# Toeplitz weights of two channels per load in 32-partition pieces, x loads and transposes moved to the front, and fewer V tasks

## The chip, the cores and the metric

The kernel runs on one core of a Trainium2 chip. The metric is the device time of one execution in microseconds (us). A core has TensorE (PE: matrix products; its weight loads are listed as PEld), VectorE (DVE), ScalarE (ACT), GpSimd (POOL) and SyncE (SP), each with its own instruction stream, and 16 DMA engines that move data between HBM and on-chip memory. Engines meet at semaphores. A DMA is issued from a queue: here mostly SP's, and also ACT's and POOL's. An engine works through its stream in order, so an instruction that waits holds up all that stand behind it. TensorE's clock has two levels, 1.2 and 2.4 GHz; the profile gives the granted clock of a stretch as a share of the higher.

## What is computed

Two independent parts whose outputs stand side by side. Part A is a long convolution over 2048 steps for each of 640 channels; part B is attention with 32 heads of width 20 over 2048 rows.

```python
# part A (S = 2048, D = 640, ks = 4)
k_shift = sum over t of k_pad[:, t:t + S, :] * shift_k[:, ks - 1 - t]
kv = k_shift * v
y = causal convolution of kv with ssm_k along S, for each channel (by FFT in the reference)
a = q * (y + kv * ssm_D)
# part B (H = 32, Dh = 20)
q, k, v = split(x @ wqkv)
p = softmax(q k^T * Dh ** -0.5)
b = (p v) @ wo
out = concatenate([a, b], axis=-1)          # all in bf16
```

## The kernel before

**Recording and queues.** The program is recorded in one Python pass: `Prog.op` and `Prog.dmas` append to an engine's list and derive semaphore waits from the buffers that a step reads and writes (`Buf`). The order of the recording is the order of each engine's stream. All DMAs pass L144, the helper, so the profile shows them under that line.

**Attention.** The work is cut into 512 blocks b: a chunk of 512 queries (qc, 4 of them), a group of four heads (g, 8), a block of 128 keys (kb, 16). For each block `S_task` (L410) makes four score matmuls (L418) into two pairs of PSUM banks out of three (banks 0 to 5), `EXP_task` (L427) takes two exponentials of 128x1024 on ScalarE (L430) into one of eight slots of `P_sb`, and `PV_task` (L437) adds P times V into bank 6 (`OBANK`, L443). After 16 blocks the sum is copied out and an N task (L455) transposes and divides it. After eight groups come T tasks (`OnT_task`, transposes L499) and O tasks (`O_task`, the output product L514).

**The loop** (L720) does for each b: the exponentials of b, the scores of b+1, P times V of b-1, and then side tasks: up to two (one from b = 48 on) from the list `pend`, which is sorted by a due time. In it are the transposes of x (X tasks, `XT_task`, L293), the projections for K and Q (`KQ_task`, L314, 20 matmuls each), the V projections (`V_task`, L333, three for each key block by the table `VZ`: 8, 12 and 12 heads), and the N, T and O tasks. From the start of the loop (`late`) all side tasks share one PSUM bank, 7 (`MISC`); ahead of it X tasks rotate through banks 2 to 5. Every fifth block from 25 on a `kv_task` makes 128 rows of kv on VectorE, from k and v rows loaded by `kst_load` and from `Ctile`, shift_k spread over all partitions. Setup gets `Ctile` on POOL's queue: an element-wise load of shift_k to four partitions, a copy to the scratch `kshT`, and a broadcast load.

**The convolution** runs from b = 124 in blocks that have no task due. It is a product with Toeplitz weights: for one step, called a channel in what follows, `hk_load` (L560) brings 128 rows of 2112 elements from `kext_scratch` (the zero-padded kernel in HBM) to a slot of `HK`. Row p of 32 rows starts p elements later in the same row of `kext`, which makes it a Toeplitz matrix; the four groups X of 32 partitions hold four channels 80 apart. There are 160 steps, five slots (`NHK`), and each slot is loaded again when its last matmul is recorded. A step has 32 matmuls (L594) with 128x128 weights out of its slot. Four steps make a batch, which ends with two copies on VectorE and four matmuls (L615, called z here), and takes six blocks: about 26, 26, 27, 28 and 21 matmuls, then L615. There are 40 batches. The moving operand `KVX` is rearranged on POOL (L571) from `KVr`, which `kvr_load` (L556) brings in twice, from rows of 160 bytes. After 20 batches `A_load` and `A_task` (L625, L632) finish half of part A.

**At the start**, SP loads x in two pieces of 512 rows into two slots of `xst`, ACT's queue issues the weights in ten DMAs (5 chunks, of 160 columns of each of K, Q and V for `b_Wa`, then of 480 for `b_Wb`), and the third and fourth piece of x are issued after the X tasks of a slot are recorded.

## Time and profile before

| what | value |
|---|---|
| median of 3 runs | 1476.86 us (1476.44 to 1484.54) |
| the profiled execution's time | 1481.97 us |
| its span, first to last instruction | 1480.1 us |
| ScalarE busy | 970.8 us, 66% |
| PE busy (matmuls) | 1015.2 us, 69% |
| VectorE busy | 273.5 us, 18% |
| DMA moved | 129.06 MB, mean 87 GB/s |
| mean granted clock | 0.671 |

The profile is one execution. Its views: the chain of work that ended last, followed back from the end; the waits, by engine and by what ended them; busy time by line; busy time in chosen stretches; instructions in order of time. "Idle before" an instruction is time in which its engine did nothing, and the name behind the arrow is what ended it. Matmuls are pipelined, so the sum over lines is more than what PE needs.

### The profile page before, as it was taken

How to read it: one execution, taken by the hardware profiler on the slowest of the kernel's cores; microseconds unless marked ns; L12 is line 12 of the kernel's file. 1: busy time of each engine (PE TensorE's matmuls, PEld its weight loads, DVE VectorE, ACT ScalarE, POOL GpSimd, SP SyncE). 2: the span in 40 equal slices, each digit the busy share in tenths (PEclk: the TensorE clock that was granted, in tenths of full speed). 3: DMA queues.
4: the chain of work that ended last, by engine and by line, in shares of the span. 5: the costliest groups of instructions: out<-in, count | busy, mean ns of one | idle time of the engine just before them, and what ended most of it. 6: DMA issues, size and time to landing. Idle time of an engine off the chain costs nothing.

```text
span 1480.1 us, 24848 instructions
## 1 busy us (share of the span) xinstructions
PE 1015.2 (69%) x11344; PEld 478.6 (32%) x11344; DVE 273.5 (18%) x570; ACT 970.8 (66%) x1027; POOL 123.9 (8%) x100
## 2 busy tenths in 40 slices
...
GB/s 143 159 1 37 88 68 91 94 72 109 72 76 106 106 107 106 106 106 106 116 103 109 104 128 109 107 106 106 106 106 106 106 106 94 83 17 1 1 0 19
DMA packets 70487, 129.06 MB, mean 87 GB/s; under 512 B 21456, under 2 KB 47182, under 8 KB 70382
## 3 DMA queue, kind: packets, MB, share of 16 engines
...
q10 hardware_dynamic: 4000, 2.46, 0.9%
q0 software_dynamic: 1056, 3.44, 0.8%
...
q14 instruction: 16, 0.13, 0.0%
...
## 4 chain that ended last, share of the span: by engine, by line
DMA 45%; PE 23%; ACT 19%; DVE 8%; SPq 3%; issue 1%; ACTq 0%; DVEq 0%
DMA R<-kext_scratch 42%; ACT P_sb L430 19%; PE PS L314 6%; PE PS L594 5%; PE PS L418 4%; PE PS L443 4%; SPq L144 3%; PE PS L514 2%; PE PS L333 2%; DVE R L364 1%; DVE R L362 1%; DVE KT L321 1%; DMA R<-kv_scratch 1%; DVE QT L321 1%; DMA R<-in_B_x_dram 1%
## 5 line engine op out<-in xcount | busy, mean ns | idle before, releaser
L430 ACT ACTIVATE P_sb<-PS 128x1024 bf16<-128x1024 f32 x1024 | 968.3, 1056 | 483.8 <-PE PS L418 474.3
L594 PE MATMUL PS<-R 128*128 128x128 bf16 (+15 forms) x5120 | 297.5, 221 | 215.3 <-DMA R<-kext_scratch 215.3
L594 PEld LDWEIGHTS PS<-R 128*128 128x128 bf16 x5120 | 262.9, 115 | 292.0 <-DMA R<-kext_scratch 223.6
L418 PE MATMUL PS<-QT,KT 20*128 20x512 bf16 x2048 | 273.6, 524 | 109.2 <-ACT P_sb L430 104.6
L443 PE MATMUL PS<-P_sb,V_sb 128*21 128x512 bf16 x2048 | 271.2, 521 | 3.7 <-DVE V_sb L338 2.5
L571 POOL COPY R<-R 32x512 bf16<-32x512 bf16 x80 | 107.2, 1339 | 724.8 <-PE PS L594 714.1
L418 PEld LDWEIGHTS PS<-QT,KT 20*128 20x128 bf16 x2048 | 54.4, 96 | 255.9 <-ACT P_sb L430 203.1
L314 PE MATMUL PS<-R 128*20 128x512 bf16 x1280 | 106.3, 475 | 44.0 <-DVE KT L321 10.9
L607 DVE CAST ZH<-PS 128x256 bf16<-128x256 f32 x40 | 17.0, 424 | 559.8 <-PE PS L594 559.8
L443 PEld LDWEIGHTS PS<-P_sb,V_sb 128*21 128x21 bf16 x2048 | 51.6, 91 | 188.2 <-issue 180.1
L451 DVE CAST OT_sb<-PS 128x512 bf16<-128x512 f32 x32 | 22.1, 691 | 293.6 <-PE PS L443 293.5
L314 PEld LDWEIGHTS PS<-R 128*20 128x20 bf16 x1280 | 32.6, 105 | 95.0 <-issue 29.9
L514 PE MATMUL PS<-Wo_sb,OnT 128*128 128x320 bf16 x160 | 39.0, 401 | 22.9 <-DVE OnT L503 18.3
L333 PE MATMUL PS<-R 128*128 128x240 bf16 (+1 forms) x240 | 35.8, 291 | 16.4 <-DVE V_sb L338 9.2
L321 DVE CAST KT<-PS 128x512 bf16<-128x512 f32 x32 | 22.1, 690 | 61.2 <-PE PS L314 61.2
L333 PEld LDWEIGHTS PS<-R 128*128 128x128 bf16 x240 | 21.3, 109 | 31.8 <-DVE V_sb L338 13.5
L321 DVE CAST QT<-PS 128x512 bf16<-128x512 f32 x32 | 22.1, 690 | 48.4 <-PE PS L314 48.4
L514 PEld LDWEIGHTS PS<-Wo_sb,OnT 128*128 128x128 bf16 x160 | 17.1, 121 | 41.8 <-DVE OnT L503 21.3
L293 PE MATMUL PS<-ident,R 128*128 128x128 bf16 x80 | 9.8, 287 | 26.1 <-DMA R<-in_B_x_dram 22.7
L549 POOL MEMSET R<- 128x2048 bf16 x2 | 3.6, 1804 | 284.3 <-DMA kvr_scratch<-R 284.2
L615 PE MATMUL PS<-ZH,Win 128*128 128x256 bf16 x80 | 23.0, 388 | 6.2 <-DVE ZH L608 6.1
L338 DVE CAST V_sb<-PS 128x240 bf16<-128x240 f32 (+1 forms) x48 | 18.3, 381 | 42.7 <-PE PS L333 42.7
...
## 6 DMA issues: line engine op xcount, KB each, us to landing
R<-kext_scratch SPq DMA_DIRECT2D x160, 528.0 KB
R<-in_A_k_dram SPq DMA_DIRECT2D x15, 640.0 KB, 3.8
R<-in_B_x_dram SPq DMA_DIRECT2D x4, 640.0 KB, 8.9
...
```

Source lines behind the costliest of these rows:

```text
L144: ins = e.dma_start(out, in_)
L314: ins = e.matmul(bank[bk][32 * i:32 * i + DH, :], W_sb[:, cc, off + i * DH:off + (i + 1) * DH], xT[:, cc, c * 512:(c + 1) * 512], start=(c ...
L321: P.op("dve", lambda e: e.tensor_copy(dstT[:, g, c * 512:(c + 1) * 512], bank[bk]), reads=[bkb[bk]], writes=[bd])
L333: ins = e.matmul(bank[bk][:, 0:w], xT[:, cc, kb * 128:(kb + 1) * 128], W_sb[:, cc, 2 * D + h0 * DH:2 * D + h0 * DH + w], start=(cc == 0), ...
L418: ins = e.matmul(bank[bk], KT[32 * u:32 * u + DH, g, kb * 128:(kb + 1) * 128], QT[32 * u:32 * u + DH, g, qc * 512:(qc + 1) * 512], start=T ...
L430: P.op("act", lambda e, pr=pr, s0=s0: e.activation(P_sb[:, pr % NPS, :], PS[:, s0 * 512:s0 * 512 + 1024], ACT.Exp, scale=scale), reads=[bk ...
L443: ins = e.matmul(bank[OBANK][32 * u:32 * u + DH + 1, :], V_sb[:, kb, 4 * g + u, :], P_sb[:, (2 * b + u // 2) % NPS, (u % 2) * 512:(u % 2) ...
L451: P.op("dve", lambda e: e.tensor_copy(OT_sb[:, i, :], bank[OBANK]), reads=[bkb[OBANK]], writes=[b_OT[i]])
L514: ins = e.matmul(bank[bk][:, 0:320], OnT[:, i, cc, :], Wo_sb[:, cc, hf * 320:(hf + 1) * 320], start=(cc == 0), stop=(cc == NCC - 1))
L571: P.op("pool", lambda e, dst=dst, src=src: e.tensor_copy(dst, src), reads=[cv["KVr"]], writes=[cv["KVX"][i]] if X == 3 else [], extra=(cv[ ...
L594: P.op("pe", lambda e, o=o, lhsT=lhsT, rhs=rhs, st=st, last=last: e.matmul(o, lhsT, rhs, start=st, stop=last, skip_group_check=True), read ...
L615: ins = e.matmul(sub(bank[MISC], [[64, 4], [1, n]], o), w, sub(a, [[64, 4], [1, n]]), start=False, stop=True, skip_group_check=True)
```

## The change

1. `HK` has three slots of two channels in place of five of one. `hk_load` is called for a pair, and issues four DMAs of 32 partitions each, whose source leads with the 32 partitions and then the two channels. A slot is loaded again after every second channel. The matmuls read the same columns.
2. All four x loads are issued at the start on SP, into four slots. ACT's queue issues the 160-column weights in three DMAs (K, Q, V), SP the 480-column ones in three after x.
3. The X tasks that are not done ahead of the loop are due in its first three blocks: up to six tasks run in each of these, without a budget. In these blocks (`late` = 1) side tasks alternate between banks 7 and 6, and P times V is held back and then made up, two at a time.
4. `VZ` has two entries (8 and 24 heads) in place of three: 32 V tasks for 48, the second kind with 480 columns.
5. `Ctile` is made on VectorE at b = 16 (`C_task`, four strided copies) from a broadcast load of shift_k into the second `kst` slot; the three POOL DMAs and the scratch `kshT` go. That slot's first k load follows C_task.
6. The first k load is cut at partition 32.

```diff
 HKW = 2112
-NHK = 5
+NHK = 3
...
-        HK_E, KVR_E, KVX_E, Y_E, AST_E = HKW, 64 * 80, 8 * 256, 16 * 320, 2 * 320
-        ph0 = NCC * S + NCC * 1920 + 2 * 4 * D + 2 * 5 * D + KS * D + 2 * D + 2 * D
+        HK_E, KVR_E, KVX_E, Y_E, AST_E = 2 * HKW, 64 * 80, 8 * 256, 16 * 320, 2 * 320
+        ph0 = NCC * S + NCC * 1920 + 4 * 4 * D + 2 * 5 * D + KS * D + 2 * D + 2 * D
...
         W_sb = carve(NCC * 1920).rearrange("p (c n) -> p c n", c=NCC)
-        xst = [carve(4 * D).rearrange("p (t d) -> p t d", t=4) for _ in range(2)]
+        xst = [carve(4 * D).rearrange("p (t d) -> p t d", t=4) for _ in range(4)]
...
         pos[0] = 0
-        HK = [carve(HK_E) for _ in range(NHK)]
+        HK = [carve(HK_E).rearrange("p (s n) -> p s n", s=2) for _ in range(NHK)]
...
         kvr_d = nc.dram_tensor("kvr_scratch", (S, D), BF16).ap()
-        kshT = nc.dram_tensor("kshT_scratch", (KS, D), BF16).ap()
...
         b_Wa, b_Wb, b_Wo, b_D = Buf(), Buf(), Buf(), Buf()
-        b_xst = [Buf(), Buf()]
+        b_xst = [Buf() for _ in range(4)]
...
         b_QT = {(qc, g): Buf() for g in range(NG) for qc in range(4)}
-        b_V = {(kb, z): Buf() for kb in range(NKB) for z in range(3)}
+        b_V = {(kb, z): Buf() for kb in range(NKB) for z in range(2)}
...
-        d_x = [DS("x0"), DS("x1")]
-
-        def x_load(n):
-            P.dma("sp", xst[n % 2], ap(x2, [[D, 128], [128 * D, 4], [1, D]], n * 512 * D), d_x[n % 2],
-                  writes=[b_xst[n % 2]])
-
-        dW = [DS("wa"), DS("wb")]
-        for z, (c0, w, bw) in enumerate(((0, 160, b_Wa), (160, 480, b_Wb))):
-            x_load(z)
-            P.dmas("act", [(ap(W_sb, [list(W_sb.ap[0]), [D, 3], [1, w]], cc * 1920 + c0),
-                            ap(B_wqkv, [[1920, 128], [D, 3], [1, w]], cc * 128 * 1920 + c0)) for cc in range(NCC)],
-                   dW[z], writes=[bw])
+        for n in range(4):
+            P.dma("sp", xst[n], ap(x2, [[D, 128], [128 * D, 4], [1, D]], n * 512 * D), DS("x%d" % n),
+                  writes=[b_xst[n]])
+        for eng, c0, w, bw in (("act", 0, 160, b_Wa), ("sp", 160, 480, b_Wb)):
+            P.dmas(eng, [(ap(W_sb, [list(W_sb.ap[0]), [1920, NCC], [1, w]], z * D + c0),
+                          ap(B_wqkv, [[1920, 128], [128 * 1920, NCC], [1, w]], z * D + c0)) for z in (1, 0, 2)],
+                   DS("w" + eng), writes=[bw])
...
         rot = [0]
-        late = [False]
+        late = [0]
...
         def mbank():
-            if late[0]:
+            if late[0] == 2:
...
             rot[0] += 1
-            return (MISC, 0, 1)[rot[0] % 3]
+            return ((MISC, OBANK, 0, 1)[rot[0] % 4], (MISC, OBANK)[rot[0] % 2])[late[0]]
...
             if late[0]:
-                bk = MISC
+                bk = mbank()
...
                 xbank[0] += 1
-            src = xst[(t // 4) % 2]
+            src = xst[t // 4]
...
                 return ins
-            P.op("pe", pe, reads=[b_xst[(t // 4) % 2], b_ident], writes=[bkb[bk]])
+            P.op("pe", pe, reads=[b_xst[t // 4], b_ident], writes=[bkb[bk]])
...
                 P.op("dve", lambda e: e.tensor_copy(dst, srcp), reads=[bkb[bk]], writes=[b_xT[t]])
-            if t % 4 == 3 and t // 4 + 2 < 4:
-                x_load(t // 4 + 2)
...
-        VZ = [(0, 8), (8, 12), (20, 12)]
+        VZ = [(0, 8), (8, 24)]
...
             if tb == 0:
-                ks = [(kst[i][KS - 1 - j:128, j, :], k2[0:128 - (KS - 1 - j), :]) for j in range(KS)]
+                ks = [(kst[i][a:e, j, :], k2[a - (KS - 1 - j):e - (KS - 1 - j), :]) for j in range(KS)
+                      for a, e in ((KS - 1 - j, 32), (32, 128))]
...
             P.op("pool", lambda e: e.memset(tB, 0.0), writes=[b_tB])
-            with nc.allow_non_contiguous_dma(reason="tiny shift_k transpose"):
-                pass
-
-            def load_skT(e):
-                with nc.allow_non_contiguous_dma(reason="tiny shift_k transpose"):
-                    return e.dma_start(tA[0:KS, :], ap(A_shift_k, [[1, KS], [KS, D]]))
-            P.op("pool", load_skT, writes=[b_tA], dsem=d_sk)
-            P.op("pool", lambda e: e.dma_start(kshT, tA[0:KS, :]), reads=[b_tA], writes=[b_kshT], dsem=d_sk)
-            P.op("pool", lambda e: e.dma_start(
-                Ctile, ap(kshT, [[0, 128], [-D, KS], [1, D]], (KS - 1) * D)), reads=[b_kshT], writes=[b_C], dsem=d_sk)
+            P.dma("sp", kst[1][:, 0:4, :], ap(A_shift_k, [[0, 128], [1, KS * D]]), d_sk, writes=[b_kst[1]])
...
             kst_load(0)
+
+        def C_task():
+            for j in range(KS):
+                src = ap(kst[1], [list(kst[1].ap[0]), [KS, D]], KS - 1 - j)
+                P.op("dve", lambda e, j=j, src=src: e.tensor_copy(Ctile[:, j, :], src), reads=[b_kst[1]], writes=[b_C])
             kst_load(1)
...
         def zof(g):
-            return 0 if g < 2 else (1 if g < 5 else 2)
+            return 0 if g < 2 else 1
...
             kvr_load(0)
-            for qd in range(NHK):
-                hk_load(qd)
+            for pr in range(NHK):
+                hk_load(pr)
...
-        def hk_load(qd):
-            B, m = divmod(qd, 80)
-            P.dma("sp", HK[qd % NHK], ap(kext, [[80 * KXL, 4], [1, 32], [1, HKW]], (320 * B + m) * KXL + 1),
-                  d_hk[qd % NHK], reads=[b_kext], writes=[cv["HK"][qd % NHK]])
+        def hk_load(pr):
+            B, m = divmod(2 * pr, 80)
+            P.dmas("sp", [(HK[pr % NHK][32 * X:32 * X + 32],
+                           ap(kext, [[1, 32], [KXL, 2], [1, HKW]], (320 * B + 80 * X + m) * KXL + 1)) for X in range(4)],
+                   d_hk[pr % NHK], reads=[b_kext], writes=[cv["HK"][pr % NHK]])
...
                     i = c % 2
-                    slot = qd % NHK
+                    slot = (qd // 2) % NHK
...
                             last = (d == 15 and r1 == 1)
-                            lhsT = HK[slot][:, 64 + 128 * d - 64 * r1:64 + 128 * d - 64 * r1 + 128]
+                            lhsT = HK[slot][:, qd % 2, 64 + 128 * d - 64 * r1:64 + 128 * d - 64 * r1 + 128]
...
                             if last:
-                                if qd + NHK < 160:
-                                    hk_load(qd + NHK)
+                                if qd % 2 == 1 and qd // 2 + NHK < 80:
+                                    hk_load(qd // 2 + NHK)
...
         for t in range(NKB):
-            add(-10 if t < 4 else t - 4, 0.45, ("X", t), lambda t=t: XT_task(t))
+            add(-10 if t < 4 else (t - 4) // 5, 0.45, ("X", t), lambda t=t: XT_task(t))
...
             add(kb, 0.4, ("V", kb, 0), lambda kb=kb: V_task(kb, 0))
-            add(26 + kb, 0.6, ("V", kb, 1), lambda kb=kb: V_task(kb, 1))
-            add(70 + kb, 0.6, ("V", kb, 2), lambda kb=kb: V_task(kb, 2))
+            add(16 + 2 * kb, 1.0, ("V", kb, 1), lambda kb=kb: V_task(kb, 1))
...
             run_best()
-        late[0] = True
+        late[0] = 1
...
                 S_task(b + 1)
-            if b >= 1:
-                PV_task(b - 1)
+            if b == 3:
+                late[0] = 2
+            for m in ([] if b < 3 else [2 * b - 6, 2 * b - 5] if b < 5 else [b - 1]):
+                PV_task(m)
             budget = 1.0
+            if b == 16:
+                C_task()
...
             if lock[0] is None:
-                cap = 2 if b < 48 else 1
-                while pend and nm < cap and budget > 0.3:
+                cap = 6 if b < 3 else (2 if b < 40 else 1)
+                while pend and nm < cap and (budget > 0.3 or b < 3):
...
                     budget -= run_best()

```

The order that results, at three places. SP's queue where the program begins, before (`R` is the on-chip region that holds xst, W_sb and kst; the shape is that of the destination):

```order
L144 DMA R<-in_B_x_dram 128x4x640 x2
L144 DMA Wo_sb<-in_B_wo_dram 128x5x640
L144 DMA Dbc<-in_A_ssm_D_dram 128x640
L144 DMA R<-in_A_k_dram 125x640
L144 DMA R<-in_A_k_dram 126x640
L144 DMA R<-in_A_k_dram 127x640
L144 DMA R<-in_A_k_dram 128x640
L144 DMA R<-in_A_v_dram 128x640
L144 DMA R<-in_A_k_dram 128x2560
L144 DMA R<-in_A_v_dram 128x640
L144 DMA R<-in_B_x_dram 128x4x640 x2
```

and now:

```order
L144 DMA R<-in_B_x_dram 128x4x640 x4
L144 DMA R<-in_B_wqkv_dram 128x5x480 x3
L144 DMA R<-in_A_shift_k_dram 128x2560
L144 DMA Wo_sb<-in_B_wo_dram 128x5x640
L144 DMA Dbc<-in_A_ssm_D_dram 128x640
L144 DMA R<-in_A_k_dram 29x640
L144 DMA R<-in_A_k_dram 96x640
```

The second pair of x loads has moved ahead of the k and v loads, and three weight loads from ACT's queue to SP's.

SP's queue where the convolution begins, before (`R<-kext_scratch` are the Toeplitz weights, `R<-kvr_scratch` the rows for KVX):

```order
L144 DMA R<-kvr_scratch 32x64x80 x4
L144 DMA R<-kext_scratch 128x1x2112 x9
L144 DMA out_dram<-Bout 128x640 x4
L144 DMA R<-kext_scratch 128x1x2112 x60
L144 DMA R<-kvr_scratch 32x64x80 x4
L144 DMA R<-kext_scratch 128x1x2112 x16
L144 DMA R<-in_A_q_dram 128x2x320
```

and now:

```order
L144 DMA R<-kvr_scratch 32x64x80 x4
L144 DMA R<-kext_scratch 32x2x2112 x20
L144 DMA out_dram<-Bout 128x640 x4
L144 DMA R<-kext_scratch 32x2x2112 x120
L144 DMA R<-kvr_scratch 32x64x80 x4
L144 DMA R<-kext_scratch 32x2x2112 x32
L144 DMA R<-in_A_q_dram 128x2x320
```

Each weight load has become half a pair's: four pieces of 32 partitions and two channels stand for two loads of 128 partitions and one.

PE's stream from its first instruction, before (L293 is a transpose of x, five to a task; L314 K or Q; L333 V; L418 scores; L443 P times V):

```order
L293 MATMUL PS<-ident,R 128x128 x20
L314 MATMUL PS<-R 20x512 x40
L418 MATMUL PS<-QT,KT 128x512 x8
L293 MATMUL PS<-ident,R 128x128 x5
L333 MATMUL PS<-R 128x160 x5
L418 MATMUL PS<-QT,KT 128x512 x4
L443 MATMUL PS<-P_sb,V_sb 21x512 x4
L293 MATMUL PS<-ident,R 128x128 x5
L333 MATMUL PS<-R 128x160 x5
L418 MATMUL PS<-QT,KT 128x512 x4
L443 MATMUL PS<-P_sb,V_sb 21x512 x4
L293 MATMUL PS<-ident,R 128x128 x10
```

and now (L287, L306, L325 and L407 are the same four steps):

```order
L287 MATMUL PS<-ident,R 128x128 x20
L306 MATMUL PS<-R 20x512 x40
L407 MATMUL PS<-QT,KT 128x512 x8
L287 MATMUL PS<-ident,R 128x128 x25
L325 MATMUL PS<-R 128x160 x5
L407 MATMUL PS<-QT,KT 128x512 x4
L287 MATMUL PS<-ident,R 128x128 x25
L325 MATMUL PS<-R 128x160 x5
L407 MATMUL PS<-QT,KT 128x512 x4
L287 MATMUL PS<-ident,R 128x128 x10
L306 MATMUL PS<-R 20x512 x20
L325 MATMUL PS<-R 128x160 x15
```

The twelve transposes that were spread over the first twelve blocks now stand in the first three, ahead of the first P times V. From block 95 on, PE's stream is the same in both.

## Rows read from the trace of the kernel before

**Rows 1.** The page's chain that ended last: shares by engine, by line.

```profile
DMA R<-kext_scratch 42%; ACT P_sb L430 19%; PE PS L314 6%; PE PS L594 5%; PE PS L418 4%; PE PS L443 4%; SPq L144 3%; PE PS L514 2%; PE PS L333 2%; DVE R L364 1%; DVE R L362 1%; DVE KT L321 1%; DMA R<-kv_scratch 1%; DVE QT L321 1%; DMA R<-in_B_x_dram 1%
```

**Rows 2.** Costliest groups: count | busy, mean ns | idle before, what ended it.

```profile
L430 ACT ACTIVATE P_sb<-PS 128x1024 bf16<-128x1024 f32 x1024 | 968.3, 1056 | 483.8 <-PE PS L418 474.3
```

**Rows 3.** Waits: who, for what: us in total, times, longest.

```profile
PE PS L594 <- DMA R<-kext_scratch: 215.3, 95, 9.5
```

**Rows 4.** Stretches: bounds, us, engines' busy (x instructions), granted clock, DMA share, GB/s.

```profile
17.45:95.06 77.61, 45.33 (x389) 18.09 (x390) 14.97 (x32) 27.03 (x28) 2.87 (x4) 0.60 0.39 82
95.06:320.75 225.69, 170.20 (x1919) 58.58 (x1917) 109.77 (x216) 152.56 (x160) 0.00 (x0) 0.84 0.22 72
...
378.18:1268.11 889.93, 624.07 (x7789) 360.18 (x7791) 106.06 (x235) 537.94 (x565) 96.43 (x72) 0.67 0.28 104
1268.11:1480.10 211.99, 134.36 (x936) 31.14 (x936) 27.35 (x58) 193.99 (x211) 0.00 (x0) 0.52 0.07 19
```

**Rows 5.** The chain in order of time, near the end: start us, us, what.

```profile
1289.60 26.70 ACT P_sb L430 x29
```

**Rows 6.** Stretches for the DMA: weights, then loads of 128 rows, then kvr.

```profile
480.00:518.00 38.00, 28.02 (x351) 16.19 (x351) 3.29 (x8) 23.05 (x24) 5.34 (x4) 0.68 0.26 106
41.00:48.00 7.00, 0.00 (x0) 0.00 (x0) 0.00 (x0) 0.00 (x0) 1.65 (x2) 0.50 0.99 346
338.00:347.20 9.20, 5.80 (x44) 1.06 (x40) 0.00 (x0) 9.20 (x12) 2.90 (x2) 0.50 1.31 148
```

**Rows 7.** Stretches: two and five convolution blocks, a mixed one, three output chains.

```profile
378.18:384.00 5.82, 5.82 (x68) 3.96 (x69) 0.00 (x0) 4.63 (x5) 0.00 (x0) 0.50 0.02 5
416.49:425.65 9.16, 8.57 (x168) 5.73 (x169) 0.59 (x2) 9.16 (x11) 0.37 (x1) 1.00 0.20 65
...
838.33:863.50 25.17, 21.61 (x326) 12.04 (x325) 12.40 (x27) 23.73 (x27) 0.00 (x0) 1.00 0.43 123
393.01:416.49 23.48, 19.69 (x126) 7.42 (x127) 5.75 (x13) 14.99 (x17) 0.00 (x0) 0.64 0.21 81
806.14:846.35 40.21, 17.19 (x124) 6.85 (x125) 9.80 (x22) 14.87 (x17) 2.02 (x2) 0.66 0.30 100
1212.28:1238.10 25.82, 22.34 (x126) 7.93 (x125) 6.16 (x13) 15.33 (x17) 0.00 (x0) 0.54 0.23 90
```

**Rows 8.** DMA issues: ns on SP min/median/max; then KB each, us to landing.

```profile
L144 SPq DMA_DIRECT2D R<-kext_scratch x160: 499/3230/5937, 342.9 to 1244.6; - x160
...
R<-in_A_k_dram SPq DMA_DIRECT2D x15, 640.0 KB, 3.8
...
R<-kshT_scratch POOLq DMA_DIRECT2D x1, 640.0 KB, 6.7
```

**Rows 9.** The chain in order of time, in the second output chain.

```profile
806.47 4.91 SPq L144
...
811.43 15.36 DMA R<-kv_scratch
```

**Rows 10.** Timeline of the start: start us, us, engine, line, instructions [idle before].

```profile
0.74 9.53 ACTq L144 DMA_DIRECT2D R<-in_B_wqkv_dram  x10
10.72 18.97 SPq L144 DMA_DIRECT2D R<-in_A_k_dram  x4
12.99 3.66 PE L314 MATMUL PS<-R 128*20 128x512 bf16 x40 [5.72 <-ACT R L301]
52.36 0.71 PE L293 MATMUL PS<-ident,R 128*128 128x128 bf16 x5 [17.70 <-DMA R<-in_B_x_dram]
55.36 0.71 PE L293 MATMUL PS<-ident,R 128*128 128x128 bf16 x5 [0.42 <-DVE V_sb L338]
```

**Rows 11.** Timeline: a copy of 640 elements; two score tasks, a block apart.

```profile
20.17 0.49 DVE L303 COPY R<-PS 128x640 bf16<-128x640 bf16 x1 [2.78 <-PE PS L293]
119.03 0.40 PE L418 MATMUL PS<-QT,KT 20*128 20x512 bf16 x4
...
121.49 0.39 PE L418 MATMUL PS<-QT,KT 20*128 20x512 bf16 x4
```

## The prediction

> **What bounds the kernel now.** I read the chain of waits first, then the waits, then the kernel stretch by stretch. In the chain [rows 1] the first name is not an engine: 42% of the span is the transfer `R<-kext_scratch`, the Toeplitz weights, and ScalarE's exponentials (L430) hold only 19%. ScalarE is still the floor: 1024 exponentials with 968.3 us busy [rows 2]. What ended its idle time is PE's score matmul L418, with 474.3 us [rows 2], and PE itself sat idle for 215.3 us before L594 until weights landed [rows 3].
>
> The stretches in [rows 4] are cut where score tasks begin: S(0) at 17.45, S(14) at 95.06, S(94) at 320.75, S(125) at 378.18, S(407) at 1268.11. ScalarE's counts there show it (two exponentials for a block of one score task). The 282 blocks with the convolution in them took 889.93 us, 3.16 us each. In the last stretch ScalarE is busy 193.99 of 211.99 us and runs 211 exponentials; from the chain, 29 of them take 26.70 us [rows 5], which is 0.92 us each and 1.84 us for a block. So the convolution costs 1.3 us a block above the floor, and that is where the time is.
>
> Why the weights are late: in a steady window of that stretch the DMA engines are busy 0.26 of 16, about 4.2 engines, and move 106 GB/s [rows 6]. One load is 128 rows of 4,224 B, 540,672 B; at 106 GB/s that is 5.1 us, and 160 of them are 86.5 MB or 816 us. Four engines are full and twelve idle. The source pattern of `hk_load` leads with a dimension of 4, `[80 * KXL, 4]`. A window with loads that lead with 128 rows on both sides shows 0.99 and 346 GB/s [rows 6].
>
> That PE keeps up when no weight is late is the second thing to read. At 416.49 five blocks with convolution took 9.16 us at a granted clock of 1.00 (2.4 GHz), ScalarE busy all of it [rows 7]: 1.83 us each, the floor. At 0.50 (1.2 GHz) two such blocks took 5.82 us [rows 7].
>
> **The change part by part.**
>
> *Weight loads.* Each pair of channels now has four transfers of 32 partitions, with 32 leading on both sides. If they spread over 16 engines, a pair (1.081 MB) takes 3.1 us at 346 GB/s; if nothing spreads, 10.2 us at 106 GB/s. PE needs a pair in at least 5.5 us: four channels fill five blocks and a sixth holds L615, 6 x 1.83 = 11.0 us for two pairs. With three slots of pairs a reload is issued when its slot's pair ends and is due two pairs, 11 us, later. It needs SP's four issues, at 0.50 us each when nothing holds them up (the least of 160; the median of 3.23 us is a full queue) [rows 8], so 2 us, and 3.1 us of transfer: hidden, with about 6 us over. The break-even rate is 86.5 MB over the 567 us found below, 153 GB/s. Nothing in this trace shows a 32-partition piece of long rows, so both ends stay in the range; I take the upper, since the only thing that sets the loads of 346 GB/s apart from these is the count of partitions, and the A_k loads, whose 5,120 B rows overlap each other as these do, land 640 KB in 3.8 us [rows 8], 172 GB/s with all fixed time in it.
>
> The Trainium skill, page "DMA: Bandwidth & Descriptors", section "Why a DMA increments its semaphore by 16 and not by 1", says that the count of DMA engines is the largest number up to 16 that divides the slowest dimension of both sides: 4 before, 16 after. The 0.26 above agrees. By it alone the sum would be the one below.
>
> *The convolution's stretch after.* 282 blocks at 1.83 us are 517 us. Above that:
> - three chains of output tasks (T and O, eight blocks each), which are unchanged in order. They took 23.48, 40.21 and 25.82 us [rows 7] against 14.67 at the floor. The first and third are the low clock and single MISC bank: +8.8 and +11.2. In the second, +25.5, the chain shows an SP wait of 4.91 us and 15.36 us of `kv_scratch` landing behind weights [rows 9]; with a queue that is not full I leave 4 us of these 20.3: +9. Together 29.
> - the first two blocks at the low clock, 5.82 against 3.66: +2.
> - the clock. In [rows 7] it held at 1.00 through 25.17 us that contain one L615 block and one N block in a row, and fell in the chain that begins at 393.01. The program's order has 18 N blocks in the stretch; I let a third of them lose it, for two blocks at +1.1: 6 x 2.2 = +13.
> - the second `kvr_load`: the first one filled the engines for 9.2 us [rows 6] (the share over 1 is a sum over queued packets), about as much as the slack, and small DMAs of A tasks: +6.
>
> So 567 us for 889.93: **-323**. Bounds: 537 (no clock lost, no DMA stall) and 816 + 25 for the old rate.
>
> *The start.* Up to S(0): the ACT queue spends 9.53 us on ten weight issues before its table load and two copies, and PE's first L314 starts at 12.99, 5.72 us after it could [rows 10]. Three issues remain on ACT, the other three go behind x on SP. I give 3.5 of the 5.72 us, the small W load then landing last; between 0 and 5.7. From S(0) to S(14): PE has the same tasks in both (12 transposes, 8 K or Q, 13 and 14 V, 13 and 14 S); it is busy 45.33 of 77.61 us [rows 4]. Of the 32 idle, 17.70 us are one wait for the third x load [rows 10], which stood on SP behind k loads that took 18.97 us to issue [rows 10]. All four x loads are now issued first: -17.7 (0 if they came late all the same, which the window at 346 GB/s [rows 6], with two of them in it, excludes). Two banks (MISC and OBANK) let a transpose run beside the copy of the one before: the idle of L293 and L333 before DVE copies is some 5 us more (twelve transposes, 0.42 at one [rows 10]); I take -5, between 0 and -16 (the rest of the idle, and a clock above 0.60). Start: **-26**, bounds -18 to -38. POOL's shift_k gather and its two copies go; no engine waits for the kext fill behind it, since the first weights are issued at 342.9 [rows 8].
>
> *The V tasks and C_task.* From S(14) to S(94) the orders of both have 54 blocks with a K or Q task. Before, 22 others hold half V tasks, after, 16 hold whole ones and 7 nothing. A block with two halves took 2.46 us at the high clock (119.03 to 121.49) [rows 11]; a whole one has five matmuls of 480 columns for ten of 240 and one copy for two, so it lies between the floor's 1.83 and 2.46, and I put it at 2.0. That saves under 5 us; C_task's four strided copies on VectorE add 2 to 3 (640 elements took 0.49 us unstrided [rows 11]), once, with PE's MISC bank behind them. I count **0**, from -8 to +5. The k load for block 1 now waits for C_task but has 14 blocks, over 25 us, until it is read. Stretches S(94) to S(125) and after S(407) are the same rows in the same order: 0.
>
> *Sum*, against the profiled span: 1480.1 - 26 - 323 = 1131.1. The profiled execution's time was 1481.97, 1.87 over its span, and 5.1 over the median of 1476.86: 1131.1 + 1.9 - 5.1 = **1128 us**.
>
> **The rivals.**
>
> *Half rate.* Two engines share whatever a 32-partition piece passes through, so 173 GB/s. A pair then takes 6.2 us for 5.5 in the densest part; 16 blocks with one N block hold five pairs, 31 us for 29.3. Eighteen times 1.8 us is 32 us, less what the output chains give back: 1128 + 25 = 1153. For it: no row shows 32 partitions of long rows. Against it: the average need of 153 GB/s is still met. The Trainium skill, page "SBUF — State Buffer", section "Door 1: The DMA port swizzle (why [64,N] ≈ [32,N])", states that 32 partitions reach 8 of 16 ports, 189 GB/s measured at 1 MiB; by that, 5.7 us a pair and a stall only in the densest part. No run here shows it yet.
>
> *The clock does not hold.* PE is full in a convolution block only at 2.4 GHz; if each L615 block lets it fall, half of the 200 convolution blocks run at the low level, +1.1 us each: 1128 + 110 - 13 = 1225. For it: the stretch's mean is 0.67 [rows 4] and the last stretch, where ScalarE is the bound, has 0.52 [rows 4]. Against it: 25.17 us at 1.00 across such blocks [rows 7]; the falls in the stretch stand beside weight waits.
>
> *Nothing spreads.* The four pieces run on as few engines as before: 106 GB/s, only the start is gained, 1477 - 26 - 10 = 1441. Against it: the leading 4 is gone on both sides.
>
> *Slower.* The 32 partitions of a piece read one row of kext shifted by 2 B each, all engines at once the same 4 KB; before, four engines read four rows. If that holds the rate under 93 GB/s, 86.5 MB take over 931 us, the stretch's 890 plus the start's gain plus 1%. At 80 GB/s: 1081 us, 1128 + 514 = 1642. Against it: `R<-kshT_scratch`, one 5 KB block read by 128 partitions at once, lands 640 KB in 6.7 us [rows 8], 98 GB/s at least.
>
> **How the numbers follow.** My forecast 0.66, half rate 0.12, clock 0.13, nothing spreads 0.05, slower 0.04. The likeliest case by itself reaches from 1088 (537 us and a start of -38) to about 1160. The range goes up to 1205, so that it holds the half rate and the milder part of the clock case: 0.66 + 0.12 + 0.04, about 0.8. A measurement of this kernel tells about 1% from no change. Faster by over 1%: the first three and most of the fourth, 0.95; within 1%: 0.02, where nothing spreads and the start gains nothing; slower 0.03.
>
> **What would show it.** In the profile after: the DMA share above 0.35 and over 150 GB/s in the convolution's slices, `R<-kext_scratch` gone from the head of the chain with L430 in its place, PE's wait before the Toeplitz line under 30 us (over 100 would be a DMA still too slow), ScalarE's busy share near 0.86, clock in the convolution above 0.8 (0.6 without weight waits is the clock rival), S(0) near 14 us and no x wait of 17 us. Wrong would be a share that stays at 0.26, or blocks of 2.9 us with no wait in them.

## The result and the profile after

The changed kernel takes 1093.47 us, the median of 4 runs (1089.22 to 1098.01); the kernel before, on the same chip, took 1476.65 us, the median of 4 (1474.82 to 1484.54). The ratio is 0.7398, with a 95% interval from 0.7356 to 0.744. The profiled execution of the kernel after spans 1093.4 us.

In the kernel after, the exponentials are L419 (L430 before), the scores L407 (L418), the Toeplitz matmuls L584 (L594), the projections for K and Q L306 (L314) and for V L325 (L333), the transposes of x L287 (L293), with their copies L297 (L303).

The chain that ended last, shares by engine and line (before: [rows 1]):

```profile
ACT P_sb L419 62%; PE PS L306 7%; PE PS L407 4%; PE PS L584 3%; PE PS L503 3%; PE PS L432 3%; PE PS L325 2%; DVE KT L313 2%; DVE R L357 2%; DVE R L355 2%; DVE QT L313 1%; DVE V_sb L330 1%; DMA R<-in_B_wqkv_dram 1%; DVE OT_sb L440 1%; DMA R<-kv_scratch 1%
```

The transfer that held 42% of the chain is no longer among its shares. The exponentials hold 62%, for 19% before.

The costliest groups (count | busy, mean ns | idle before, what ended it), the answer to [rows 2] and [rows 3]:

```profile
L419 ACT ACTIVATE P_sb<-PS 128x1024 bf16<-128x1024 f32 x1024 | 950.5, 1145 | 119.2 <-PE PS L407 112.6
...
L584 PE MATMUL PS<-R 128*128 128x128 bf16 (+15 forms) x5120 | 220.4, 196 | 6.1 <-DMA R<-kext_scratch 4.3
```

ScalarE's idle time before the exponentials went from 483.8 to 119.2 us at about the same busy time, and PE's wait for weights from 215.3 us in 95 waits to 4.3 us.

The stretches, cut at the same score tasks as [rows 4]: bounds, us, busy of PE, PEld, DVE, ACT and POOL (x instructions), granted clock, DMA share, GB/s:

```profile
0.00:16.43 16.43, 5.97 (x61) 3.40 (x62) 4.30 (x8) 2.69 (x3) 8.56 (x15) 1.00 0.93 309
16.43:53.82 37.39, 31.12 (x399) 15.02 (x399) 15.60 (x34) 26.59 (x28) 0.00 (x0) 0.95 0.39 140
53.82:265.40 211.58, 160.93 (x1827) 49.57 (x1825) 111.63 (x209) 153.37 (x161) 0.00 (x0) 0.88 0.25 80
265.40:323.38 57.98, 36.80 (x256) 7.26 (x256) 7.67 (x17) 57.05 (x63) 14.29 (x10) 0.50 0.50 95
323.38:881.51 558.13, 480.09 (x7788) 287.05 (x7789) 107.13 (x235) 519.46 (x565) 95.98 (x72) 0.93 0.74 165
881.51:1093.40 211.89, 135.14 (x936) 31.21 (x936) 27.35 (x58) 194.00 (x211) 0.00 (x0) 0.52 0.07 19
```

| stretch | before | after | change |
|---|---|---|---|
| to S(0) | 17.45 | 16.43 | -1.0 |
| S(0) to S(14) | 77.61 | 37.39 | -40.2 |
| S(14) to S(94) | 225.69 | 211.58 | -14.1 |
| S(94) to S(125) | 57.43 | 57.98 | +0.6 |
| S(125) to S(407), with the convolution | 889.93 | 558.13 | -331.8 |
| after S(407) | 211.99 | 211.89 | -0.1 |

In the convolution's stretch the DMA share went from 0.28 to 0.74 and the rate from 104 to 165 GB/s, and the clock from 0.67 to 0.93. A dense window of the same view shows what the new transfers can do at most:

```profile
417.00:424.00 7.00, 5.90 (x109) 3.73 (x105) 1.27 (x3) 7.00 (x9) 5.34 (x4) 1.00 1.04 221
```

All 16 engines are busy and move 221 GB/s. The loads of 128 rows in [rows 6] moved 346 GB/s at 0.99. A pair of channels, 1.081 MB, thus takes 4.9 us, not the 3.1 us of the forecast.

### The profile page after: what moved, and what is told of

It reads as the page before. It is cut to its first block, busy times and chain, and to the rows that moved or that the text cites. A ratio compares the mean times of both kernels' runs of the same rounds, so it can differ in the third digit from the quotient of the medians.

```text
span 1093.4 us, 24833 instructions
## 1 busy us (share of the span) xinstructions
PE 850.1 (78%) x11264; PEld 393.5 (36%) x11264; DVE 273.7 (25%) x558; ACT 953.2 (87%) x1027; POOL 118.8 (11%) x97
## 4 chain that ended last, share of the span: by engine, by line
ACT 62%; PE 23%; DVE 11%; DMA 2%; issue 1%; SPq 0%; ACTq 0%
ACT P_sb L419 62%; PE PS L306 7%; PE PS L407 4%; PE PS L584 3%; PE PS L503 3%; PE PS L432 3%; PE PS L325 2%; DVE KT L313 2%; DVE R L357 2%; DVE R L355 2%; DVE QT L313 1%; DVE V_sb L330 1%; DMA R<-in_B_wqkv_dram 1%; DVE OT_sb L440 1%; DMA R<-kv_scratch 1%
## 5 line engine op out<-in xcount | busy, mean ns | idle before, releaser
L419 ACT ACTIVATE P_sb<-PS 128x1024 bf16<-128x1024 f32 x1024 | 950.5, 1145 | 119.2 <-PE PS L407 112.6
L407 PE MATMUL PS<-QT,KT 20*128 20x512 bf16 x2048 | 240.5, 459 | 150.9 <-ACT P_sb L419 145.0
L432 PE MATMUL PS<-P_sb,V_sb 128*21 128x512 bf16 x2048 | 239.1, 459 | 1.2 <-ACT P_sb L419 1.2
L584 PE MATMUL PS<-R 128*128 128x128 bf16 (+15 forms) x5120 | 220.4, 196 | 6.1 <-DMA R<-kext_scratch 4.3
L584 PEld LDWEIGHTS PS<-R 128*128 128x128 bf16 x5120 | 197.2, 99 | 53.2 <-issue 48.7
L407 PEld LDWEIGHTS PS<-QT,KT 20*128 20x128 bf16 x2048 | 53.2, 94 | 301.0 <-ACT P_sb L419 254.4
L306 PE MATMUL PS<-R 128*20 128x512 bf16 x1280 | 94.0, 430 | 37.1 <-DVE KT L313 11.1
L306 PEld LDWEIGHTS PS<-R 128*20 128x20 bf16 x1280 | 29.9, 98 | 82.6 <-DVE QT L313 19.1
L325 PE MATMUL PS<-R 128*128 128x160 bf16 (+1 forms) x160 | 29.1, 316 | 13.7 <-DVE KT L313 5.8
L313 DVE CAST KT<-PS 128x512 bf16<-128x512 f32 x32 | 22.1, 690 | 44.5 <-PE PS L306 44.5
L313 DVE CAST QT<-PS 128x512 bf16<-128x512 f32 x32 | 22.1, 690 | 43.7 <-PE PS L306 43.7
L507 DVE CAST Bout<-PS 128x320 bf16<-128x320 f32 x32 | 15.7, 491 | 37.7 <-PE PS L503 37.2
L453 PE MATMUL PS<-ident,OT_sb 128*128 128x128 bf16 x128 | 14.7, 246 | 13.1 <-DVE OT_sb L440 12.8
L357 DVE TENSOR_TENSOR R<-R 128x640 bf16<-128x640 bf16 x48 | 23.6, 492 | 1.6
L355 DVE TENSOR_TENSOR R<-R 128x640 bf16<-128x640 bf16 x48 | 23.5, 490 | 1.1
```

The source lines that it names most:

```text
L306: ins = e.matmul(bank[bk][32 * i:32 * i + DH, :], W_sb[:, cc, off + i * DH:off + (i + 1) * DH], xT[:, cc, c * 512:(c + 1) * 512], start=(c ...
L313: P.op("dve", lambda e: e.tensor_copy(dstT[:, g, c * 512:(c + 1) * 512], bank[bk]), reads=[bkb[bk]], writes=[bd])
L325: ins = e.matmul(bank[bk][:, 0:w], xT[:, cc, kb * 128:(kb + 1) * 128], W_sb[:, cc, 2 * D + h0 * DH:2 * D + h0 * DH + w], start=(cc == 0), ...
L355: P.op("dve", lambda e, j=j: e.tensor_tensor(tB, k[:, j, :], Ctile[:, j, :], ALU.mult), reads=[b_kst[i], b_C], writes=[b_tB])
L357: P.op("dve", lambda e: e.tensor_tensor(tA, tA, tB, ALU.add), reads=[b_tA, b_tB], writes=[b_tA])
L407: ins = e.matmul(bank[bk], KT[32 * u:32 * u + DH, g, kb * 128:(kb + 1) * 128], QT[32 * u:32 * u + DH, g, qc * 512:(qc + 1) * 512], start=T ...
```

## The experiments

**Theories.** Mine: the gain in the convolution comes from the leading dimension of the source, 32 in place of 4, which brings 16 engines to the loads in place of four; the pairing and the depth of the slots add little. Rival: it comes from the pairs, that is, from longer loads and other slots. Second question: why do full engines move 221 and not 346 GB/s, and does it cost anything? Third: which edit gave the start's 41 us and the 14 us behind it?

Each kernel was executed once, with a profile, and the last one four times. Kernels are named by what was done to them. The kernel after was not executed again beside them; stretches that an edit doesn't touch show how well single executions agree. S(14) to S(94) has the same rows in the kernel after, after_lead4, wide_rows, two_slots, front_one_bank and out_steps, and took 210.0 to 213.3 us in these six. The convolution has the same rows in the kernel after, after_spread, front_one_bank, after_v3 and kv_thin, and took 555.0 to 558.4 us in these five.

**hk_only** is the kernel before with the first item of the change alone:

```diff
-NHK = 5
+NHK = 3
-            P.dma("sp", HK[qd % NHK], ap(kext, [[80 * KXL, 4], [1, 32], [1, HKW]], (320 * B + m) * KXL + 1), ...
+            P.dmas("sp", [(HK[pr % NHK][32 * X:32 * X + 32],
+                           ap(kext, [[1, 32], [KXL, 2], [1, HKW]], (320 * B + 80 * X + m) * KXL + 1)) for X in range(4)], ...
```

> The kernel before with the weight loads of the change alone (pairs, 32-partition pieces, three slots). If the loads are the whole of the convolution's gain: its 282 blocks take about 558 us as in the changed kernel, for 890 before, and the time is 1477 - 332 = 1145 us. If the changed start or the V tasks had a part in it (by another clock or another place of SP's queue), more than 1165 us.

It took 1140.64 us; the kernel before took 1472.34 beside it. The convolution's stretch:

```profile
374.74:927.00 552.26, 475.88 (x7788) 285.77 (x7789) 107.16 (x235) 519.21 (x565) 96.06 (x72) 0.94 0.74 167
```

It took 552.26 us, with the start and the stretch to S(14) as before (17.48 and 77.16 us). So the weight loads give the convolution's whole gain by themselves; the front and the merged V tasks give the rest, and the two add.

**pieces_only** is the kernel before with four pieces, but one channel for a load and five slots:

```diff
-            P.dma("sp", HK[qd % NHK], ap(kext, [[80 * KXL, 4], [1, 32], [1, HKW]], (320 * B + m) * KXL + 1), ...
+            P.dmas("sp", [(HK[qd % NHK][32 * X:32 * X + 32],
+                           ap(kext, [[1, 32], [1, HKW]], (320 * B + 80 * X + m) * KXL + 1)) for X in range(4)], ...
```

> The kernel before with one channel a load and five slots as they were, but each load in four pieces of 32 partitions. Theory of the spread over engines: the DMA rate in the convolution rises to about 180 GB/s as in the changed kernel and the time is about 1145 us. Rival, that pairs and the deeper lookahead (six channels for five) gave the gain: the rate stays at 106 GB/s and the time at about 1470 us.

It took 1142.11 us, and its convolution 548.5 us, no longer than with pairs. A steady window of it, same columns as above:

```profile
420.00:458.00 38.00, 33.66 (x617) 21.32 (x614) 5.86 (x13) 38.00 (x43) 10.70 (x8) 1.00 0.70 179
```

So neither the pairs nor going from five slots of one channel to three of two matter for the time; the pieces do.

**after_lead4** is the kernel after with pairs loaded by two DMAs of 128 partitions that lead with 4, as before:

```diff
-            P.dmas("sp", [(HK[pr % NHK][32 * X:32 * X + 32],
-                           ap(kext, [[1, 32], [KXL, 2], [1, HKW]], (320 * B + 80 * X + m) * KXL + 1)) for X in range(4)],
+            P.dmas("sp", [(HK[pr % NHK][:, s, :],
+                           ap(kext, [[80 * KXL, 4], [1, 32], [1, HKW]], (320 * B + m + s) * KXL + 1)) for s in range(2)],
```

> The changed kernel with each pair loaded by two DMAs of 128 partitions whose source leads with 4 groups, as before the change. Theory of the spread: DMA share 0.26 and 106 GB/s in the convolution, 890 us for its blocks, so 1093 + 332 = 1425 us. Rival, pairs and lookahead: about 1093 us.

It took 1427.43 us. Its convolution and a steady window:

```profile
322.25:1213.82 891.57, 576.06 (x7790) 344.73 (x7791) 105.20 (x234) 530.81 (x565) 95.76 (x72) 0.75 0.27 103
400.00:438.00 38.00, 25.88 (x372) 16.11 (x372) 3.98 (x9) 24.46 (x26) 5.32 (x4) 0.80 0.26 106
```

The convolution takes 891.57 us again, for 889.93 before, and share and rate are the 0.26 and 106 GB/s of [rows 6] to the digit. PE waited 236.1 us for weights in 59 waits. With pieces_only this settles the first question: the leading dimension is the whole cause, and the rival on pairs falls. That the pieces come as four DMAs for one is not it either: wide_rows, next, spreads with a single DMA. The Trainium skill, page "DMA: Bandwidth & Descriptors", section "Why a DMA increments its semaphore by 16 and not by 1", gives 4 engines for a leading 4 and 16 for a leading 32; the traces agree (0.26 of 16 engines is 4.2, and shares near 1 with 32).

**wide_rows** is the kernel after with one DMA of 128 partitions for a pair, all from one row of kext, each partition 2 B further on. The weights of three of the four channel groups are therefore others than the reference's; bytes, rows and matmuls are as many as before:

```diff
-            P.dmas("sp", [(HK[pr % NHK][32 * X:32 * X + 32],
-                           ap(kext, [[1, 32], [KXL, 2], [1, HKW]], (320 * B + 80 * X + m) * KXL + 1)) for X in range(4)],
-                   d_hk[pr % NHK], ...
+            P.dma("sp", HK[pr % NHK], ap(kext, [[1, 128], [KXL, 2], [1, HKW]], (320 * B + m) * KXL + 1),
+                  d_hk[pr % NHK], ...
```

> The changed kernel with each pair loaded by one DMA that leads with 128 partitions, all reading one row of kext shifted by 2 B each; the weights of three of the four channel groups are therefore others than the reference has, with the same bytes moved. In the changed kernel a packet of 4,224 B takes 316 ns for 164 before. Theory that a 32-partition piece is narrow at the on-chip side: packets fall back to about 164 ns, the share from 0.8 to about 0.42, time 1085 to 1093 us. Rival, that 16 engines reading one row of HBM hinder each other: packets stay near 316 ns or get longer, share 0.8 or more.

It took 1087.77 us. Its convolution, and the window that stands above for the kernel after:

```profile
326.06:874.89 548.83, 477.22 (x7788) 284.36 (x7789) 107.27 (x235) 519.10 (x565) 96.18 (x72) 0.94 0.53 168
417.00:424.00 7.00, 6.10 (x116) 3.79 (x112) 1.27 (x3) 6.94 (x9) 2.21 (x2) 1.00 0.64 200
```

The stretch moves the same bytes (168 GB/s for 165) with 0.53 of the engines in place of 0.74. The records of single packets say it more sharply: the median packet of 4,224 B of the weights takes 164 ns here, in the kernel before and in after_lead4, all of which write 128 partitions in one DMA, and 313 to 314 ns in the kernel after and hk_only (268 ns in pieces_only), which write 32. Sixteen packets in 314 ns are 215 GB/s, in 164 ns 412; the 3 us from 558.5 on in wide_rows do move 397 GB/s, at a share of 1.03. All rows overlapping in one row of HBM cost nothing here, so the slow packet comes from the 32 partitions of a piece and not from the overlap of the source rows. Nor is such a packet slow by itself: those with no other packet in flight at their middle take a median of 172 ns in the kernel after (46 packets) and 164 ns in pieces_only (95). It is the engines beside each other on such pieces that slow one another. This costs the kernel little: 548.83 us against the 555.0 to 558.4 of the five kernels above, 6 to 10 us, and pieces_only took 548.5 with slow packets too. One execution of each can't tell how much of it is real.

**x_first** is the kernel before with its four x loads ahead of everything else on SP, into four slots:

```diff
+            x_load(2 * z)
+            x_load(2 * z + 1)
-            x_load(z)
-            if t % 4 == 3 and t // 4 + 2 < 4:
-                x_load(t // 4 + 2)
```

> The kernel before with all four x loads issued first, into four slots, and nothing else. The start from S(0) to S(14) took 77.6 us before and 37.4 us in the changed kernel. My step (the 17.7 us wait goes, little else): 60 us, so about 1460 us in all. Rival, that without the wait PE's clock stays at its high level there, which shortens everything: 45 us or less, and about 1445 us.

It took 1466.54 us beside 1477.02 for the kernel before. S(0) to S(14):

```profile
20.27:82.56 62.29, 47.18 (x389) 18.41 (x390) 14.99 (x32) 27.03 (x28) 2.87 (x4) 0.86 0.57 100
```

The stretch fell from 77.61 to 62.29 us, -15.3. But S(0) stands at 20.27 for 17.45: PE's first projection starts at 15.03 for 12.99, after a wait of 7.67 us for a copy of x on ACT, which stands behind its ten weight issues (11.56 us here, 9.53 before), and its 40 matmuls take 4.45 us for 3.66. So 2.8 us are given back, and x first is worth 12.5 us alone.

**after_spread** is the kernel after with the X tasks due one for a block, side tasks in bank 7 alone and P times V in every block, as before:

```diff
-            add(-10 if t < 4 else (t - 4) // 5, 0.45, ("X", t), lambda t=t: XT_task(t))
+            add(-10 if t < 4 else t - 4, 0.45, ("X", t), lambda t=t: XT_task(t))
-        late[0] = 1
+        late[0] = 2
-            for m in ([] if b < 3 else [2 * b - 6, 2 * b - 5] if b < 5 else [b - 1]):
-                PV_task(m)
+            if b >= 1:
+                PV_task(b - 1)
-                cap = 6 if b < 3 else (2 if b < 40 else 1)
+                cap = 2 if b < 40 else 1
```

> The changed kernel with the twelve transposes spread over the first twelve blocks again, side tasks in one bank and P times V one block behind, as before. If the front of transposes in two banks is what the start gained beyond the x wait: S(0) to S(14) takes about 58 us for 37.4, and the time is near 1114 us. If it was the wait and the clock that follows: about 42 us, and 1098 us.

It took 1123.71 us. S(0) to S(14), and S(14) to S(94):

```profile
16.55:78.45 61.90, 47.01 (x390) 18.48 (x391) 14.98 (x32) 27.03 (x28) 0.00 (x0) 0.60 0.23 83
78.45:294.50 216.05, 162.69 (x1840) 50.41 (x1837) 113.66 (x213) 153.13 (x160) 0.00 (x0) 0.87 0.25 80
```

The first is x_first's 62.3 us again. So the dense front is worth 61.90 - 37.39 = 24.5 us there: PE's busy time falls by 15.9 us at a clock of 0.95 for 0.60, and its idle time by 8.6. It may be worth another 4.5 us in the stretch behind (216.05 to 211.58), or 3 to 6 against the six kernels above (210.0 to 213.3).

**front_one_bank** keeps the dense front but leaves its side tasks in bank 7:

```diff
-        late[0] = 1
+        late[0] = 2
         S_task(0)
```

> The changed kernel with its transposes in the first three blocks, but all side tasks in bank 7 from the start. S(0) to S(14) took 37.4 us with two banks and 61.9 us with the transposes spread, where the granted clock stayed at its low level from 18 to 59 us. If PE's dense stretch, and the clock that it keeps, is what the front gained: 40 to 44 us. If it is the second bank: near 55 us.

It took 1109.93 us. S(0) to S(14), and two windows of it:

```profile
16.41:69.73 53.32, 39.51 (x399) 17.71 (x399) 16.02 (x34) 26.59 (x28) 0.00 (x0) 0.71 0.27 97
```

```profile
40.00:45.00 5.00, 4.16 (x30) 1.99 (x29) 0.98 (x3) 0.67 (x1) 0.00 (x0) 0.50 0.00 0
...
50.00:55.00 5.00, 4.19 (x62) 1.92 (x66) 1.53 (x4) 3.55 (x4) 0.00 (x0) 1.00 0.00 0
```

The density alone gives 8.6 of the 24.5 us, the second bank the other 15.9. Without it PE waits, before nine of the twelve tasks with transposes, for the copy of the one before: its idle time before L287 is 5.5 us in this kernel and 0.6 us in the kernel after. Of the 15.9 us, 7.5 are idle time of all lines (13.8 to 6.3) and 8.4 are PE's busy time (39.51 to 31.12). The busy time goes with the clock, which stayed low to about 48.9 us here: PE is as busy in both small windows, and starts 30 matmuls in the first and 62 in the second.

**after_v3** is the kernel after with three V tasks for a key block again:

```diff
-        VZ = [(0, 8), (8, 24)]
+        VZ = [(0, 8), (8, 12), (20, 12)]
-            add(16 + 2 * kb, 1.0, ("V", kb, 1), lambda kb=kb: V_task(kb, 1))
+            add(26 + kb, 0.6, ("V", kb, 1), lambda kb=kb: V_task(kb, 1))
+            add(70 + kb, 0.6, ("V", kb, 2), lambda kb=kb: V_task(kb, 2))
```

> The changed kernel with the three V tasks for each key block of before, due as before. S(14) to S(94) took 225.7 us before and 211.6 in the changed kernel; I had forecast no difference. If the merged V tasks are the cause: about 225 us there, and 1107 us in all. If something else of the change is (C_task's place, the denser start that leaves fewer tasks after block 14): 212 us and 1093.

It took 1101.19 us. S(14) to S(94):

```profile
56.15:274.38 218.23, 162.61 (x1887) 56.38 (x1887) 109.83 (x217) 152.68 (x161) 0.00 (x0) 0.87 0.24 78
```

With 218.23 for 211.58 us the merged V tasks are worth 6.6 us there (5 to 8 against the six kernels above). With the front's 4.5, 11 of the 14.1 us are found. The other 3 us may be spread between executions: hk_only and x_first show 222.7 us in this stretch, whose rows in them are those of the kernel before and pieces_only with their 225.7.

**two_slots** is the kernel after with two slots of pairs (`NHK = 2` for 3).

> The changed kernel with two pair slots for three, so that a reload is due one pair, about 5.5 us, after it is issued. A pair needs SP's four issues (2 us) and 256 packets of 316 ns over 16 engines (5.1 us) and some latency, so PE waits some 2 to 3 us for each of 77 pairs, and the clock falls in these waits: 1250 to 1350 us. If the loads came faster than that (the 3.1 us of my forecast's rate), under 1150 us.

It took 1142.61 us, far less than I had expected. The convolution and PE's wait:

```profile
325.86:929.42 603.56, 504.06 (x7788) 305.67 (x7788) 107.33 (x235) 524.68 (x565) 95.84 (x72) 0.87 0.69 155
```

```profile
PE PS L584 <- DMA R<-kext_scratch: 35.7, 33, 5.2
```

The stretch grew by 45.4 us, of which 35.7 us are 33 waits for weights. Outside the output chains a pair comes every 6.5 us, for 5.9 us in the kernel after, and a wait is 1.1 us on average; I had expected 2 to 3 us for each of 77 pairs. The forecast gave a reload 5.5 us. In the kernel after a median of 6.8 us pass between the last matmul of a pair and the first of the pair after next, and a load takes about 7.1 us here, 1.7 from its first to the end of its fourth issue and 5.4 to landing: with two slots it is late by little, and only behind some pairs. The third slot is worth these 45 us; the rest of the convolution's gain, some 286 us, doesn't need it.

**kv_thin** tries what the chain of the kernel after shows next. In its stretch from S(14) to S(94), in order of time on VectorE and then on PE (start us, us, engine, line, instructions [idle before]):

```profile
97.88 0.49 DVE L355 TENSOR_TENSOR R<-R 128x640 bf16<-128x640 bf16 x1
98.41 0.49 DVE L357 TENSOR_TENSOR R<-R 128x640 bf16<-128x640 bf16 x1
98.93 0.49 DVE L358 TENSOR_TENSOR R<-R 128x640 bf16<-128x640 bf16 x1
99.34 0.68 DVE L313 CAST KT<-PS 128x512 bf16<-128x512 f32 x1
```

```profile
100.08 2.18 PE L325 MATMUL PS<-R 128*128 128x480 bf16 x5 [2.65 <-DVE KT L313]
```

A kv_task's operations of 0.49 us stand in a row on VectorE; a copy of K behind them is late, PE waits 2.65 us for its bank, and its next five matmuls take 2.18 us (the same five took 1.19 us in kv_thin, without such a wait). The edit records a kv_task's operations one or two in a block, behind the block's side tasks:

```diff
-            if b >= 24 and b % 5 == 0 and kv_next[0] < NKB:
-                kv_task(kv_next[0])
-                kv_next[0] += 1
+            for _ in range(0 if b < 18 else (1 if b < 44 else 2)):
+                next(kv_it, None)
```

> The changed kernel with kv_task's eight VectorE operations given out one at a time behind each block's side tasks from block 18, two from block 44, in place of eight at once in every fifth block. In the changed kernel 16 such blocks took about 5.0 us for 2.06 in S(14) to S(94), with a colder block behind many. If K's and Q's copies behind the eight are what costs there: S(14) to S(94) about 165 us for 211.6, and 1047 us in all. If VectorE's total is the bound, little changes: over 1080 us.

It took 1053.97 us. S(14) to S(94):

```profile
55.69:225.24 169.55, 146.86 (x1827) 46.84 (x1827) 111.55 (x217) 153.68 (x161) 0.00 (x0) 0.95 0.32 103
```

That is 169.55 us for 211.58, 2.1 us for a block, with the same work, so the copies behind the eight operations were what cost, and not VectorE's total; the other stretches stayed (557.1 us in the convolution).

**out_steps** takes the output chains apart: T and O tasks are due three blocks for each quarter, one for a block, and not in a row of eight with one kind:

```diff
-                    add(b0 + 12, 0.4, ("T", qc, qt), lambda qt=qt: OnT_task(qc, qt))
+                    add(b0 + 12 + (3 * qt if qc < 3 else 0), 0.4, ("T", qc, qt), lambda qt=qt: OnT_task(qc, qt))
-                        add(b0 + 16 + 8 * qt + 4 * hf, 0.7, ("O", qc, qt, hf),
+                        add(b0 + 13 + 3 * qt + hf if qc < 3 else b0 + 16 + 8 * qt + 4 * hf, 0.7, ("O", qc, qt, hf),
```

> The changed kernel with the T and O tasks of the first three query chunks due in the order T, O, O, one to a block, so that no T task forces two O tasks into its block. The three output chains took 23.3, 25.2 and 23.9 us over eight blocks; in twelve blocks at the floor they take 22 us but do away with four blocks that the convolution now has later at no cost: 1093 - 25 = 1068 us. If the clock falls in them all the same (2.5 us a block): about 1085 us.

It took 1072.79 us. The convolution:

```profile
322.46:859.91 537.45, 457.17 (x7524) 273.09 (x7525) 104.61 (x228) 518.97 (x565) 96.08 (x72) 0.95 0.75 167
```

That is 537.45 us for 558.13, though some 264 of its matmuls left this stretch for the last one, which took 193.5 us to its last score task, for 194.1 in the kernel after.

**both_thin** has both edits.

> The changed kernel with both: kv_task's operations given out one or two to a block, and T and O tasks one to a block. If both gains stand, and add up: about 1022 us. If one of them is lost to the other's room on VectorE or the clock: 1045 to 1070 us.

It took 1032.1 us, the median of 4 runs (1030.04 to 1033.64), a ratio to the kernel before (1477.26, median of 7) of 0.6992, with a 95% interval from 0.6971 to 0.7013. It beats both kernels. From S(14) to S(94), to S(125) and to S(407):

```profile
54.99:224.47 169.48, 146.82 (x1826) 46.80 (x1826) 111.53 (x217) 153.67 (x161) 0.00 (x0) 0.95 0.32 103
224.47:282.45 57.98, 36.82 (x256) 7.29 (x258) 4.07 (x9) 57.04 (x63) 14.27 (x10) 0.50 0.48 85
282.45:817.60 535.15, 455.02 (x7525) 271.99 (x7526) 104.65 (x228) 518.84 (x565) 96.20 (x72) 0.96 0.75 168
```

Its span is 1028.2 us, 65.2 under that of the kernel after; the two edits alone gave 41.2 and 22.4, so they add up.

## Why the prediction was right, and where it was not

The forecast span was 1131.1 us and the measured one 1093.4, 37.7 us less: 15.2 of these stand ahead of S(14), 14.1 between S(14) and S(94), and 8.8 in the convolution; the two other stretches took 0.4 us more. The first two fell beyond the bounds that I had given them. The range still held the result, but its low end leaned on 537 us for the convolution, which its terms don't give: without the clock's 13 and the second kvr load's 6 they come to 548. That the 1093 lie inside is in part luck.

**What bounds the kernel.** Right, and shown: four engines carried the weights (after_lead4 has the convolution's old time, share and rate back, with all else changed), and ScalarE's floor was next.

**The rate of the pieces.** Wrong. I took 346 GB/s and 3.1 us a pair, because only the count of partitions set these loads apart from others; that count is what halves the rate. The row shows 221 GB/s, 4.9 us. The half-rate rival has the mechanism that the packets bear out (about 314 ns side by side, 164 to 172 ns alone), but its price was not right: I had put it at 173 GB/s, 6.2 us a pair, more than the 5.5 us that PE leaves; 4.9 us still fits. The Trainium skill, page "SBUF — State Buffer", section "Door 1: The DMA port swizzle (why [64,N] ≈ [32,N])", lets 32 partitions reach half of the ports, with 189 GB/s measured at 1 MiB and about 218 as a limit for partitions 0 to 31. The traces come close to its limit: 221 GB/s here at full engines, for pieces at all four places, and 397 where all 128 are written (wide_rows). What saved the forecast is that the break-even (153 GB/s) was worked out apart from the rate.

**The convolution, 558.1 for 567 us.** The floor of 517 held. The three output chains took:

```profile
337.87:361.14 23.27, 19.49 (x124) 7.42 (x125) 5.72 (x13) 14.98 (x17) 0.00 (x0) 0.63 0.18 47
592.94:618.12 25.18, 17.53 (x124) 6.87 (x124) 9.68 (x22) 14.88 (x17) 1.39 (x2) 0.73 0.43 113
833.74:857.68 23.94, 21.09 (x127) 7.78 (x126) 6.45 (x14) 15.07 (x17) 0.00 (x0) 0.57 0.18 47
```

Together 72.4 us, 28.4 over their floor of 44.0, against 29. One by one they are 8.6, 10.5 and 9.3 for 8.8, 9 and 11.2, so the sum fits better than its terms. In the second VectorE waited 4.67 us for the transfer of kv rows, where I had left 4. The first two blocks gave 2.0, as forecast. The clock and the second kvr load are seen on PE in order of time (start us, us, engine, line, instructions [idle before]); every block begins with L407. A window of 2 us with its granted clock, 0.50, stands behind them:

```profile
466.66 0.40 PE L453 MATMUL PS<-ident,OT_sb 128*128 128x128 bf16 x4
467.84 0.40 PE L407 MATMUL PS<-QT,KT 20*128 20x512 bf16 x4 [0.78 <-ACT P_sb L419]
468.16 0.40 PE L432 MATMUL PS<-P_sb,V_sb 128*21 128x512 bf16 x4
468.49 1.80 PE L584 MATMUL PS<-R 128*128 128x128 bf16 x26
470.22 0.61 PE L407 MATMUL PS<-QT,KT 20*128 20x512 bf16 x4
...
472.66 0.40 PE L407 MATMUL PS<-QT,KT 20*128 20x512 bf16 x4
...
555.86 0.40 PE L407 MATMUL PS<-QT,KT 20*128 20x512 bf16 x4
...
561.29 1.45 PE L584 MATMUL PS<-R 128*128 128x128 bf16 x15 [4.33 <-DMA R<-kext_scratch]
562.67 0.61 PE L407 MATMUL PS<-QT,KT 20*128 20x512 bf16 x4
...
565.50 0.61 PE L407 MATMUL PS<-QT,KT 20*128 20x512 bf16 x4
```

```profile
470.00:472.00 2.00, 2.00 (x28) 1.09 (x26) 0.00 (x0) 1.65 (x3) 0.00 (x0) 0.50 0.37 76
```

At 466.66 stands an N task, and PE is idle for 0.78 us behind it; then the clock is low from 468.7 to 472.1, and the two blocks that hold this take 4.82 us (467.84 to 472.66) for a floor of 3.66. The same excess of about 1.1 us is at four more places, begun at 492.52, 689.90, 714.65 and 809.04, each behind an N task. So the clock fell about as often as forecast, at five of 18 places for six, but a fall costs 1.1 and not 2.2 us, since only part of two blocks lies at the low level: 6 us for 13. At the second kvr load two blocks take 9.64 us (555.86 to 565.50) for 3.66: 6.0, as forecast. So 517 + 28.4 + 2.0 + 6 + 6 = 559.

**The start, -41.2 for -26, beyond its bound of -38.** Three terms, each off. S(0) came at 16.43, not near 14 (at 16.4 to 17.3 in the other kernels with this start): of 3.5 us expected I got at most 1.0, because the first projection now waits for its weights to land and not for their issue.

```profile
11.98 3.65 PE L306 MATMUL PS<-R 128*20 128x512 bf16 x40 [4.09 <-DMA R<-in_B_wqkv_dram]
```

The x wait was there for the taking, -15.3 for -17.7 in that stretch (x_first). The two banks and the dense front, which I put at -5, gave -24.5. I had counted idle time alone, and named a clock above 0.60 as a bound without a price; 15.9 of the 24.5 us are PE's busy time at the higher clock. This step was mis-sized fivefold. Its bound of 16 was too narrow: 14.6 of these are the remaining idle time, so it left 1.4 us for the clock. With it the three terms' ends make 39, not the 38 that I gave.

**S(14) to S(94), -14.1 for 0, beyond -8.** The merged V tasks gave 6.6 (after_v3), where I had 5 and set C_task against it; no run takes C_task out, so its price is not known. The front gave some 4.5 more here (after_spread), which the sum didn't have: I had treated the stretches as apart. About 3 us are not explained, and are no more than the spread between executions.

**The rivals.** Half rate: its mechanism was there, its cost not. Nothing spreads: after_lead4 shows what that would have been, 1427.43 us for 1441. The clock: 0.93 in the convolution, so it holds there. Slower: the overlap of all rows in one HBM row costs nothing (wide_rows, 164 ns for a packet as with four rows).

**What would show it.** Share 0.74 and 165 GB/s (above 0.35 and 150), the transfer gone from the chain's head, 4.3 us of waits (under 30), ScalarE busy 87% (near 86), clock 0.93 (above 0.8), the x wait of 17 us gone (the 5.6 us until the first x lands stay): as named. S(0) near 14: missed.
